# A spatial bias added by TensorE instead of VectorE, with the gate product moved from GpSimd to VectorE

## The chip, the cores and the metric

The kernel runs on one core of one Trainium2 chip. The metric is the device time of one execution in microseconds (us). Of the kernel before, three runs are shown: 330.44, 331.29 and 336.69 us, median 331.29. One further execution was profiled; it took 327.45 us, of which 325.7 us lie between its first and its last instruction (the span).

The engines that matter are TensorE (PE: matmuls; PEld: its weight loads), VectorE (DVE), ScalarE (ACT), GpSimd (POOL), and SyncE's queue (SP), which issues nearly all DMAs. Each engine carries out its instructions in order.

## The reference

Three blocks follow each other, each in float32, for a batch of 2 with 768 positions and a model width of 320:

1. an mLSTM attention (8 heads of 40) with exponential gates, computed in the kernel in 6 chunks of 128 positions for each batch;
2. a gated MLP with a spatial product, the block that is changed:

```
h = relu(x @ w_in);  u, v = h[..., :512], h[..., 512:]
v_n = (v - mean(v)) / sqrt(var(v) + 1e-6)
v_s = einsum('ts,bsd->btd', w_spatial, v_n) + b_spatial[None, :, None]
out = (u * v_s) @ w_out
```

3. a channel mix: two blends of x with its predecessor in time, `k = relu(xk @ w_k)**2`, `sigmoid(xr @ w_r) * (k @ w_v)`.

The bias `b_spatial` belongs to an output position t and is the same for every batch and channel.

## The kernel before, in words

**High and low parts.** Matmuls take operands of a type (float32r) that holds less than a float32. Every operand is therefore kept as a high part (a rounding copy, made on ScalarE) and a low part (the value minus the high part, made by the helper `sub` in line 232 on VectorE or GpSimd). A product is then three matmuls: high by high, high by low, low by high. Weights that arrive as raw bits go through `widen` (lines 248 to 286): a step on ScalarE (L269), three on VectorE (L270, L274, L278), the high part on ScalarE (L285), the low part on GpSimd (L232).

**Stages.** The attention runs chunk by chunk; in its gaps the v and u halves of the first product of block 2 are computed, as "fillers". `vpart` leaves the normalised v as `vn` (high and low), `upart` leaves u transposed as `ut`. When the last chunk is through, the pool `at` of the attention is released (line 964), and two pools take its memory over: `rk`, with 3 buffers "sq" and 11 buffers "gk" (`gated`), and `r1`, with `b_sb` (the bias, broadcast to 128 partitions) and the second half of w_spatial.

**The spatial stage** is written out in line 1084: `'h s0 K1 s1 r o0 K0 s2 v x o1 s3 o2'`. `s0` to `s3` are the groups g (batch g // 2, half g % 2 of the output positions, 384 of them). A group has four chunks d of 128 channels, and `spatial(g, d)` gives each one PSUM bank of 128 channels by 384 positions: 6 blocks of input positions, three products each, 18 matmuls. `after` queues the chain of the gate: add the bias (VectorE, L999), multiply by u (GpSimd, L1000), high part (ScalarE, L1001), low part (VectorE, L232). `o0` to `o3` are `wout(g)`, the output projection of a group into a page `x2`; `K0`, `K1`, `r` and `v` queue the widening of w_k, w_r and w_v; `x` makes the blend xk of group 0. After that come, for each group, `kpart` (tiles kp, k), rp and vv; `wout(3)` stands after the fourth `kpart` of group 0.

**What sets the order.** A planner runs in Python while the kernel is built. It keeps a clock for TensorE and a time at which each other engine comes free (`free`), gives every step of a chain a cost in us, and issues the step that can start first; `use` books time on an engine for an instruction issued outside of a chain. The result is a fixed order on TensorE, ScalarE, VectorE and GpSimd. SP's DMAs are ordered by the framework. The planner's costs are estimates: a real wait on one engine does not move the order on another. Work of `widen` counts as late and steps back behind chains that are ready.

**Memory.** There are 8 PSUM banks; a matmul into a bank waits until the bank's last reader is through. Pages ("pg", 12 of them) are handed round: a page for `x2` may be one from which `vn` is still read.

Of the kernel before, what the change touches and what calls it, by code (L numbers as in the profile page):

```python
# [7 lines left out]
F32 = mybir.dt.float32  # L8
F32R = mybir.dt.float32r
# [4 lines left out]
ALU = mybir.AluOpType  # L14
# [3 lines left out]
def tile_mlstm_gmlp_channelmix(  # L18
# [26 lines left out]
    P = 128  # L45
    H, D = 8, 40
    DA = D + 1
    B, S = 2, 768
# [4 lines left out]
    HF = 384  # L53
# [4 lines left out]
    vec, act, pool, pe = nc.vector, nc.scalar, nc.gpsimd, nc.tensor  # L58
# [64 lines left out]
    def use(e, cost, t=None):  # L123
        free[e] = max(free[e], clock[0] if t is None else t) + cost
        return free[e]
# [44 lines left out]
    def chain(key, *steps, ready=None):  # L170
        running.append(Chain(key, steps, clock[0] + 0.2 if ready is None else ready, 0.0))

    def finish(*keys, stall=True):
        for k in keys:
            while any(b[0] == k or b[0][0] == k for b in back):
                if not force_feed():
                    break
            for c in [c for c in running if c.has(k)]:
                while c in running and c.has(k):
                    advance(c.start(), skip=c)  # L180
                    if not c.open():
                        finish(split[0], stall=False)
                    if c in running and c.has(k):
                        issue(c)
        if stall:
            at_least(max([done.get(k, 0.0) for k in keys], default=0.0))
# [18 lines left out]
    def own(tag, bufs, *keys):  # L205

        h = owners.setdefault(tag, [])
        if len(h) >= bufs:
            finish(*h[-bufs], stall=tag in ("at", "mm"))
        h.append(list(keys))  # L210
# [20 lines left out]
    def sub(eng, out, a, b):  # L231
        eng.tensor_tensor(out=out, in0=a, in1=b.bitcast(F32), op=ALU.subtract)  # L232
# [82 lines left out]
    def load_qk(i):  # L315
        b, c = divmod(i, NCH)
        t = at.tile([P, 2, 4, P], F32, tag="qk", name=f"qk{i}", bufs=2)
        for hh in range(2):
            e = load(t[64 * hh:64 * hh + D], qk[b, c, hh], 164)
        st["q", i], st["k", i] = t[:, 0], t[:, 1]  # L320
        st["at", i] = e
# [11 lines left out]
    def load_o(u):  # L333
        b, j = divmod(u, 2)
        o = at.tile([P, 3, DM], F32, tag="og", name=f"og{u}", bufs=3)
        load(o, o_tok[b, j], 480)
        st["o", u] = o
# [13 lines left out]
    for a in 'i f d o2 o0 q'.split():  # L351
        dict(f=lambda: sync.dma_start(out=fg, in_=f_gate), i=lambda: sync.dma_start(out=ig, in_=i_gate),
             d=lambda: sync.dma_start(out=id_sb, in_=ident), o=lambda: load_o(int(a[1])), q=lambda: load_qk(SEQ[0]))[a[0]]()
# [290 lines left out]
    def mm_bank(name, *keys):  # L644
        if closing:
            closing.append(0)
            if len(closing) % 4:
                return bank(psa, "at", name, *keys)
        return bank(psm, "mm", name, *keys)
# [3 lines left out]
    ut = {}  # L653
# [268 lines left out]
    while todo:  # L922
        p = todo[0]["p"]
# [46 lines left out]
    def gated(name):  # L970
        return rk.tile([P, 2, HF], F32R, tag="gk", name=name, bufs=11)

    r1 = tc.alloc_tile_pool(name="r1", bufs=1, side="right", reuse_waits="tile")
    b_sb = r1.tile([P, S], F32, name="b_sb")
    sync.dma_start(out=b_sb, in_=b_sp)
    x2 = {}
    gts = {}

    def run(prs, out, after, first=(), cost=0.16):
        for t in mm3([out], prs, after, first, cost):  # L980
            t[0]()

    def spatial(g, d):
        b, hf = divmod(g, 2)
        prs = []
        for s in range(NCH):
            v0, v1 = (t[:, s % 3, d * P:(d + 1) * P] for t in vn[2 * b + s // 3])
            w = W["sp", hf][s // 3]
            w0, w1 = w[:, 0, s % 3, :], w[:, 1, s % 3, :]
            prs += [(v0, w0), (v0, w1), (v1, w0)]  # L990

        def after(ps):
            own("sq", 3, ("gt", g, d))
            vs = rk.tile([P, HF], F32, tag="sq", name=f"vs{g}_{d}", bufs=3)
            gt = gated(f"gt{g}_{d}")
            sl = slice(hf * HF, (hf + 1) * HF)
            finish(*[("ut", b, 3 * b + j, d) for j in range(3)], stall=False)
            chain(("gt", g, d),
                  ("V", 0.47, lambda: vec.tensor_tensor(out=vs, in0=ps, in1=b_sb[:, sl], op=ALU.add), ("sp", g, d)),  # L999
                  ("P", 0.96, lambda: pool.tensor_tensor(out=vs, in0=vs, in1=ut[b][:, d, sl], op=ALU.mult)),  # L1000
                  ("A", 0.41, lambda: act.copy(gt[:, 0], vs)), ("V", 0.47, lambda: sub(vec, gt[:, 1], vs, gt[:, 0])))  # L1001
            gts[g, d] = gt

        run(prs, mm_bank(f"spp{g}_{d}", ("sp", g, d))[:, :HF], after, [f"w_sp{hf}"] + [("vn", NCH * b + s) for s in range(NCH)])
# [62 lines left out]
    def sp_run(g):  # L1067
        for d in range(4):
            spatial(g, d)
# [39 lines left out]
    for g in range(2 * B):  # L1109
# [8 lines left out]
        for j in range(3):  # L1118
            sl = slice(j * P, (j + 1) * P)
# [6 lines left out]
        for j in range(3):  # L1126
            sl = slice(j * P, (j + 1) * P)
            prs = []
# [119 lines left out]
```

## Time and profile before

| | us |
|---|---|
| runs shown (3) | 330.44, 331.29, 336.69 |
| median | 331.29 |
| the profiled execution | 327.45 |
| its span | 325.7 |
| TensorE busy | 302.4 (93%) |
| VectorE busy | 224.3 (69%) |
| ScalarE busy | 163.2 (50%) |
| GpSimd busy | 145.6 (45%) |

Times in the rows below are us from the start of the span. A timeline row gives start, duration, engine, line and operation, the tiles (written <- read), shape and count; in square brackets stands how long the engine had been idle just before and what released it. Matmuls are pipelined, and the durations of several overlap: the pitch of a row of matmuls is its duration divided by its count. The granted clock of TensorE has two levels, 1.2 and 2.4 GHz, shown as 0.50 and 1.00.

### The profile page before, as it was taken

The numbers are of one execution on the slowest core, as the hardware profiler recorded it, in microseconds if no ns is written. First come the engines' busy times: TensorE is split into PE (matmuls) and PEld (weight loads), VectorE is DVE, ScalarE is ACT, GpSimd is POOL, SyncE is SP. The second block draws the span as 40 slices with busy tenths as digits, with TensorE's granted clock in tenths as the row PEclk, the third lists the DMA queues.
The fourth block names the chain that finished last, engine by engine and source line by source line (L and its number), as shares of the span: only waits on it lengthen the run. The fifth ranks groups of instructions, "written<-read, shape, count | busy, mean of one in ns | idle before, by whom it ended". The sixth has DMA issues, their size and how long they took to land.

```text
span 325.7 us, 5486 instructions
## 1 busy us (share of the span) xinstructions
PE 302.4 (93%) x1982; PEld 281.5 (86%) x1982; DVE 224.3 (69%) x430; ACT 163.2 (50%) x336; POOL 145.6 (45%) x185
## 2 busy tenths in 40 slices
PE   5979988999999999899999999449999999999995
PEld 3676866989989989799999999339999999999995
DVE  6679698958689656654997929996565745645611
ACT  4542644685466342742455316458874844753620
POOL 4133457935758644853464631655502502501500
PEclk9969997999999999999999999987999999999999
DMA  5763942353443213244115211410001001001001
GB/s 181 248 174 124 344 135 85 109 169 105 163 132 112 84 49 104 89 155 139 42 40 193 83 40 40 122 42 2 0 22 41 2 20 40 2 20 42 0 20 42
DMA packets 12854, 28.97 MB, mean 89 GB/s; under 512 B 2099, under 2 KB 6187, under 8 KB 12827
## 3 DMA queue, kind: packets, MB, share of 16 engines
q1 hardware_dynamic: 12795, 28.56, 27.5%
q8 instruction: 16, 0.26, 0.3%
q14 instruction: 11, 0.09, 0.1%
q0 software_dynamic: 32, 0.07, 0.1%
HBM read 26.35 MB, written 1.97 MB: 87 GB/s over the span
## 4 chain that ended last, share of the span: by engine, by line
PE 74%; DVE 10%; ACT 5%; POOL 4%; DMA 3%; issue 2%; SPq 1%; DVEq 0%; ACTq 0%; POOLq 0%
PE spp L612 14%; PE vv L612 13%; PE kp L612 12%; PE vp L612 6%; PE wop L612 5%; PE up L612 5%; PE av L541 5%; PE rp L612 4%; PE sc L444 3%; DMA w_inv<-in_w_in_dram 2%; PE ld L453 2%; DVE wbits L274 2%; PE wp L348 2%; PE ip L525 2%; PE sp L491 1%
## 5 line engine op out<-in xcount | busy, mean ns | idle before, releaser
L1101 POOL TENSOR_TENSOR sq<-sq 128x384 f32<-128x384 f32 x32 | 27.2, 852 | 60.3 <-ACT sq L1100 60.3
L612 PE MATMUL spp<-wsp,vn 128*128 128x384 f32 x288 | 51.0, 335 | 1.5 <-POOL vn L232 0.9
L612 PEld LDWEIGHTS spp<-wsp,vn 128*128 128x128 f32 x288 | 49.8, 188 | 2.2 <-POOL vn L232 1.2
L612 PE MATMUL kp<-xk,wk 128*128 128x384 f32 x256 | 45.9, 336 | 4.6 <-DVE vs L999 4.6
L612 PEld LDWEIGHTS kp<-xk,wk 128*128 128x128 f32 x256 | 44.4, 188 | 5.2 <-DVE vs L999 5.2
L612 PE MATMUL vv<-wv,k 128*128 128x320 f32 x288 | 43.4, 310 | 0.1
L612 PEld LDWEIGHTS vv<-wv,k 128*128 128x128 f32 x288 | 42.4, 188 | 0.6 <-DVE k L232 0.3
L232 DVE TENSOR_TENSOR k<-sq,k 128x384 fp32r<-128x384 f32 x32 | 25.7, 802 | 21.7 <-ACT k L1102 21.7
L612 PE MATMUL vp<-w_v,xg 128*128 128x512 f32 x96 | 29.3, 422 | 2.3 <-ACT xg L603 1.4
L612 PE MATMUL up<-xg,w_u 128*128 128x256 f32 x192 | 31.2, 293 | 0.0
L612 PE MATMUL wop<-gt,wo 128*128 128x384 f32 x128 | 25.7, 358 | 4.5 <-DVE vs L999 2.9
L612 PEld LDWEIGHTS wop<-gt,wo 128*128 128x128 f32 x128 | 24.1, 203 | 5.7 <-ACT wv L285 3.2
L1000 POOL TENSOR_TENSOR vs<-vs,u 128x384 f32<-128x384 f32 x16 | 20.5, 1281 | 14.2 <-DVE vs L999 14.2
L612 PEld LDWEIGHTS up<-xg,w_u 128*128 128x128 f32 x192 | 26.2, 190 | 0.5
L541 PEld LDWEIGHTS av<-kvq,dt 128*128 128x128 f32 x192 | 25.7, 203 | 0.7
L541 PE MATMUL av<-kvq,dt 128*128 128x41 f32 x192 | 25.3, 284 | 0.0
L1100 ACT ACTIVATE sq<-kp 128x384 f32<-128x384 f32 x32 | 15.4, 491 | 15.4 <-PE kp L612 15.4
L274 DVE SCALAR_TENSOR_TENSOR wbits<-wsq,wbits 128x320 int32<-128x320 int32 (+1 forms) x27 | 21.3, 793 | 2.5 <-ACT wsq L269 2.1
L612 PEld LDWEIGHTS vp<-w_v,xg 128*128 128x128 f32 x96 | 17.5, 194 | 5.8 <-DVE xg L232 1.5
L466 DVE TENSOR_TENSOR dt<-dt,sc 128x512 f32<-128x512 f32 x24 | 16.2, 682 | 7.7 <-ACT dt L463 4.5
L1140 DVE TENSOR_TENSOR ob<-rs,vv 128x320 f32<-128x320 f32 x12 | 5.8, 487 | 20.7 <-PE vv L612 20.7
L463 ACT ACTIVATE dt<-ld 128x512 f32<-128x512 f32 x24 | 14.1, 597 | 9.2 <-PE ld L455 6.1
(160 smaller groups left out, 560.3 us busy)
## 6 DMA issues: line engine op xcount, KB each, us to landing
kvq<-in_kvq_dram SPq DMA_DIRECT2D x10, 516.0 KB
qk<-in_qk_dram SPq DMA_DIRECT2D x24, 160.0 KB
wraw<-in_w_k_dram SPq DMA_DIRECT2D x6, 512.0 KB
wraw<-in_w_v_dram SPq DMA_DIRECT2D x8, 320.0 KB
wraw<-in_w_sp_dram SPq DMA_DIRECT2D x12, 192.0 KB
og<-in_o_tok_dram SPq DMA_DIRECT2D x4, 480.0 KB
out_dram<-ob SPq DMA_DIRECT2D x12, 160.0 KB
w_inv<-in_w_in_dram SPq DMA_DIRECT2D x3, 512.0 KB
```

The source lines that it names most:

```text
L232: eng.tensor_tensor(out=out, in0=a, in1=b.bitcast(F32), op=ALU.subtract)
L274: vec.scalar_tensor_tensor(out=t["bits"], in0=t["sq"].bitcast(I32), scalar=3, in1=t["bits"], op0=ALU.logical_shift_left, op1=ALU.bitwise_or)
L348: pe.matmul(wp[:, :256], junk[:, :P], junk, start=True, stop=True)
L444: pe.matmul(st["sc", i, x][:, h * P:(h + 1) * P], k_[64 * x:64 * x + D, h, :], q_[64 * x:64 * x + D, h, :], start=True, stop=True)
L453: pe.matmul(ld, lts[c % 2][:, b], rl[:, hh * 512:(hh + 1) * 512], start=True, stop=not early)
L463: ("A", 0.48, lambda: act.activation(out=d2, in_=ld, func=AF.Exp), ("e", i, hh)),
L466: ("V", 0.6, lambda: vec.tensor_tensor(out=d2, in0=d2, in1=sc, op=ALU.mult)))
L541: pe.matmul(av[:, 4 * hh + h, :], A[:, h, :], vt[:, 4 * hh + h, :], start=True, stop=True)
L612: pe.matmul(out[0], l, x, start=j == 0, stop=j == len(prs) - 1)
L1000: ("P", 0.96, lambda: pool.tensor_tensor(out=vs, in0=vs, in1=ut[b][:, d, sl], op=ALU.mult)),
L1100: chain(("k2", g, f), ("A", 0.37, lambda: act.activation(out=sq, in_=ps, func=AF.Relu), ("kp", g, f)), ("P", 0.96, lambda: pool.tensor_ten ...
L1101: ("P", 0.96, lambda: pool.tensor_tensor(out=sq, in0=sq, in1=sq, op=ALU.mult)),
```

## The change

The bias becomes a 19th matmul of every chunk. Its moving operand is `bm`, 128 rows of 768 positions: the first 64 rows hold the high part of the bias, the last 64 rows the low part. Its stationary operand `sel` is 1/64 everywhere, so that the sum over the 128 rows is high part plus low part, for each of the 128 channels. `b_sb` is loaded into the first "gk" buffer; ScalarE makes the high part for all rows, VectorE subtracts it in the lower 64 rows. VectorE multiplies the PSUM bank by u directly; GpSimd has no step in the chain any more. The two calls of `use` book 0.85 and 0.9 us in the planner.

```diff
     r1 = tc.alloc_tile_pool(name="r1", bufs=1, side="right", reuse_waits="tile")
-    b_sb = r1.tile([P, S], F32, name="b_sb")
+
+
+    b_sb = gated("b_sb").rearrange("p w t -> p (w t)").bitcast(F32)
+    bm = r1.tile([P, S], F32R, name="bm")
+    sel = r1.tile([P, P], F32R, name="sel")
     sync.dma_start(out=b_sb, in_=b_sp)
+    pool.memset(sel.bitcast(F32), 1.0 / 64)
+    act.copy(bm, b_sb)
+    sub(vec, bm[64:], b_sb[64:], bm[64:])
+    use("A", 0.85)
+    use("V", 0.9)
     x2 = {}
     gts = {}
...
             prs += [(v0, w0), (v0, w1), (v1, w0)]
+        prs.append((sel, bm[:, hf * HF:(hf + 1) * HF]))
...
             chain(("gt", g, d),
-                  ("V", 0.47, lambda: vec.tensor_tensor(out=vs, in0=ps, in1=b_sb[:, sl], op=ALU.add), ("sp", g, d)),
-                  ("P", 0.96, lambda: pool.tensor_tensor(out=vs, in0=vs, in1=ut[b][:, d, sl], op=ALU.mult)),
+                  ("V", 0.55, lambda: vec.tensor_tensor(out=vs, in0=ps, in1=ut[b][:, d, sl], op=ALU.mult), ("sp", g, d)),
                   ("A", 0.41, lambda: act.copy(gt[:, 0], vs)), ("V", 0.47, lambda: sub(vec, gt[:, 1], vs, gt[:, 0])))
```

## Rows read from the trace of the kernel before

**Rows 1.** Page, part 1: busy us, share of the span, instructions of TensorE

```profile
PE 302.4 (93%) x1982; PEld 281.5 (86%) x1982; DVE 224.3 (69%) x430; ACT 163.2 (50%) x336; POOL 145.6 (45%) x185
```

**Rows 2.** Page, part 4: the chain of waits, by engine

```profile
PE 74%; DVE 10%; ACT 5%; POOL 4%; DMA 3%; issue 2%; SPq 1%; DVEq 0%; ACTq 0%; POOLq 0%
```

**Rows 3.** Timeline, TensorE, start of the spatial stage

```profile
133.85 2.77 PE L612 MATMUL spp<-wsp,vn 128*128 128x384 f32 x15
...
137.27 0.62 PE L612 MATMUL spp<-wsp,vn 128*128 128x384 f32 x2 [0.65 <-ACT vn L681]
...
138.75 21.43 PE L612 MATMUL spp<-wsp,vn 128*128 128x384 f32 x122 [0.87 <-POOL vn L232]
```

**Rows 4.** Timeline, TensorE alone, group 2 and the output projection of group 3

```profile
166.44 12.64 PE L612 MATMUL spp<-wsp,vn 128*128 128x384 f32 x72
...
216.29 1.72 PE L612 MATMUL wop<-gt,wo 128*128 128x384 f32 x6 [2.94 <-DVE vs L999]
...
220.27 6.19 PE L612 MATMUL wop<-gt,wo 128*128 128x384 f32 x25 [0.93 <-DVE gt L232]
```

**Rows 5.** Timeline, ScalarE and VectorE at the release of x2

```profile
195.41 0.48 ACT L1018 COPY x<-wop 64x384 f32<-64x384 f32 x1 [6.69 <-PE spp L612]
...
195.92 0.55 DVE L1019 TENSOR_TENSOR x<-x,wop 64x384 f32<-64x384 f32 x1 [6.77 <-ACT x L1018]
...
197.03 0.55 DVE L232 TENSOR_TENSOR gt<-vs,gt 128x384 fp32r<-128x384 f32 x1
```

**Rows 6.** Timeline, SP: issue of b_sb's transfer

```profile
138.00 0.43 SPq L975 DMA_DIRECT2D b_sb<-in_b_sp_dram  x1
```

**Rows 7.** Stretches: us; busy PE, PEld, DVE, ACT, POOL; PEclk, DMA share, GB/s

```profile
138.00:140.50 2.50, 1.75 (x10) 1.75 (x11) 0.95 (x1) 0.62 (x4) 2.42 (x5) 1.00 0.74 243
140.50:142.50 2.00, 2.00 (x13) 2.00 (x12) 0.94 (x1) 1.86 (x4) 1.45 (x2) 1.00 0.00 0
```

**Rows 8.** Timeline, ScalarE and GpSimd, last steps of the attention's vn

```profile
140.49 0.62 ACT L681 CAST vn<-vr 128x512 fp32r<-128x512 f32 x1 [1.88 <-DVE vr L679]
...
141.19 1.31 POOL L232 TENSOR_TENSOR vn<-vr,vn 128x512 fp32r<-128x512 f32 x1 [0.55 <-ACT vn L681]
```

**Rows 9.** Tile vs: count, duration ns min/median/max, first and last start

```profile
L999 DVE TENSOR_TENSOR vs<-spp,b_sb x16: 543/546/558, 143.4 to 215.6; 128x384 f32<-128x384 f32 x16
L1000 POOL TENSOR_TENSOR vs<-vs,u x16: 1007/1293/1462, 144.1 to 216.8; 128x384 f32<-128x384 f32 x16
L1001 ACT CAST gt<-vs x16: 495/512/520, 146.3 to 218.1; 128x384 fp32r<-128x384 f32 x16
```

**Rows 10.** Timeline, a wider cast on ScalarE and a subtraction of 768 columns

```profile
198.91 1.16 ACT L1044 CAST xk<-tm 128x1152 fp32r<-128x1152 f32 x1 [0.57 <-DVE tm L1040]
...
226.01 0.96 DVE L232 TENSOR_TENSOR xr<-tm,xr 128x768 fp32r<-128x768 f32 x1 [0.44 <-ACT xr L1044]
```

**Rows 11.** Timeline of 211 to 222, VectorE and GpSimd, w_v split and gate

```profile
211.76 1.20 POOL L1000 TENSOR_TENSOR vs<-vs,u 128x384 f32<-128x384 f32 x1 [1.20 <-DVE vs L999]
212.01 1.30 DVE L278 SCALAR_TENSOR_TENSOR wsq<-wraw,wbits 128x320 int32<-128x320 int32 x1
...
213.82 0.49 DVE L278 SCALAR_TENSOR_TENSOR wsq<-wraw,wbits 128x320 int32<-128x320 int32 x1
...
214.23 0.98 DVE L270 TENSOR_SCALAR wbits<-wraw 128x320 int32<-128x320 int32 x1
...
215.60 0.55 DVE L999 TENSOR_TENSOR vs<-spp,b_sb 128x384 f32<-128x384 f32 x1
...
219.66 0.55 DVE L232 TENSOR_TENSOR gt<-vs,gt 128x384 fp32r<-128x384 f32 x1
```

**Rows 12.** Stretches, columns as in rows 7

```profile
53.10:56.40 3.30, 3.30 (x20) 2.69 (x17) 3.13 (x7) 1.12 (x2) 2.25 (x4) 0.50 0.01 3
213.50:216.80 3.30, 0.51 (x3) 0.54 (x4) 3.20 (x6) 2.04 (x5) 1.97 (x2) 1.00 0.33 99
217.00:223.60 6.60, 5.03 (x15) 4.12 (x14) 5.51 (x11) 5.20 (x12) 3.00 (x4) 0.50 0.01 4
```

## The prediction

> **What bounds the kernel now.** I read the busy shares first: TensorE is busy for 302.4 us of the span of 325.7 [rows 1]. The chain of waits agrees, with TensorE at 74% and VectorE at 10% [rows 2]. So an added matmul costs its whole pitch nearly everywhere, and the question is where the VectorE tenth lies. The timelines show two regimes around the change.
>
> Up to 203 us the spatial stage is TensorE's. After its last wait at 138.75 it runs without a gap, 72 spatial matmuls in 12.64 us [rows 3, 4], a pitch of 0.176 us.
>
> Then the bound changes hands. ScalarE's copy into x2 of group 1 waits 6.69 us and is let go at 195.41 by a spatial matmul of group 3, nine before that group's end: x2's page is one that the spatial products still read. VectorE stands behind it, idle for 6.77 us [rows 5]. When both are let go, VectorE has 24 us of queued work, does it almost without a pause, and TensorE waits for its PSUM banks (2.94 us at 216.29) and for the last split of the gate, running freely again from 220.27 [rows 4]. I call 195.4 to 220.3 the VectorE stretch. The change touches both sides.
>
> **The change, part by part**
>
> *Sixteen more matmuls*, one per group and half-chunk, each 128x384 like the others: 16 x 0.176 = **+2.8 us**. TensorE is the bound there, so nothing covers them; their weight load is one more in a stream whose loads already overlap.
>
> *The preparation of the bias, and its new wait.* Before, b_sb was needed only by VectorE's first addition. Now the 19th matmul of the first group needs bm, made by a DMA, a ScalarE cast and a VectorE subtraction. TensorE's order is fixed, so all products queue behind that one. When does it ask? The first 15 matmuls start at 133.85, two at 137.27, the 18th at 138.75 [rows 3], so the 19th is up at 138.93. When is bm there? The b_sb transfer is issued at 138.00, behind a w_sp transfer in SP's queue [rows 6]; the DMA engines are 0.74 busy to 140.50 and at 0.00 afterwards [rows 7], so it has landed by 140.50. I keep that time: the new buffer is again one of a pool that opens after the attention's last instructions. ScalarE then casts the last vn from 140.49 to 141.11 [rows 8]. The copy of 128x768 follows: 0.51 us for 384 columns [rows 9], 1.16 for 1152 [rows 10], so 0.84, done at 141.9. The subtraction of 768 columns takes 0.96 [rows 10], done at 142.9 if nothing holds it. But GpSimd's vn subtraction runs from 141.19 to 142.50 [rows 8], and a VectorE operation that meets GpSimd here takes until GpSimd's end and most of its own time: 1.30 us against 0.49 for the same form [rows 11]. That puts bm at 143.4. TensorE waits from 138.93 to 143.4: **+4.5 us** (between 4.0, without the collision, and 5.5, with 1 us more for the transfer). No later slack takes it up, since TensorE has no gap until 203.
>
> The Trainium skill ("SBUF — State Buffer", Who interferes with whom) states the same as an exclusive lock: a VectorE instruction with two SBUF inputs blocks against a GpSimd instruction that reads SBUF. By it the later of the two times holds; without it the sum would be 0.5 us less.
>
> The sel memset on GpSimd comes behind that vn subtraction, at 142.5, and has 0.9 us before bm is ready. If it were slower it would be the late one. The w_sp casts and splits of the second half queue behind copy and subtraction, about 2 us later; their products begin 72 matmuls after the first half's, and these are themselves 4.5 us later: nothing.
>
> *What the pause does to TensorE's clock.* In 53.1 to 56.4 the granted clock was 0.50 for 3.3 us; after a stretch with TensorE idle in 2.8 of 3.3 us it was 0.50 for 6.6 us [rows 12]. A 4.5 us pause is nearest to the second, which followed the longer idleness; part of the slow time falls into the pause itself, so I take 5 us of matmuls at half speed, which loses **+2.5 us** (0.9 to 3.3).
>
> The Trainium skill ("TensorE: Matmul & The Clock Gate", HAM oscillation) speaks against this change: it charges a gap in the matmul stream a slow restart on top. Without that the sum would be 2.5 us lower; rows 12 side with the rule.
>
> *The addition becomes a multiplication on VectorE*, again one PSUM and one SBUF input of 128x384. The addition took 543 to 558 ns in all 16 cases [rows 9], also where GpSimd was busy: **0** (within 0.02 each).
>
> *GpSimd loses 16 products* of 1.0 to 1.46 us [rows 9]. In the spatial stage this shortens only a chain that nobody waits for. In the VectorE stretch four remain, and each collides with a step of the w_v split, as in the product at 211.76 with the step at 212.01 [rows 11]; the four excesses are 0.64 to 0.83 us, the one shown 0.81. Three lie ahead of what TensorE waits for: **-2.3 us** (0 if the w_v subtractions of GpSimd move into the freed place and collide there; -3.1 for all four).
>
> *Order on VectorE.* The planner writes each engine's order. Without the GpSimd step the cast and the split of a gate follow their multiplication about 1.1 us sooner in its plan. The split of group 2's last chunk, at 197.03 [rows 5], then comes ahead of the wait for x2, where VectorE is idle: **-0.5 us**. At the end, the last addition starts at 215.60 and the last gate's split at 219.66, with four operations and a GpSimd product between [rows 11]; TensorE starts 0.6 us after the split starts. Directly behind one operation and ScalarE's 0.51 us cast the split would end about 2.2 us after the multiplication starts; now it ends 4.6 us after. **-2.5 us** (0 to -3.5). What is late next is TensorE's own queue: 25 products of the output projection and 32 of kp, about 10 us, then rp, whose input VectorE makes after the same stretch.
>
> *Sum against the profiled execution* (327.45 us; span 325.7 and 1.75 around it): 2.8 + 4.5 + 2.5 - 2.3 - 0.5 - 2.5 = +4.5, so 331.9. The runs shown have a median of 331.29 us, 3.8 above the profiled execution; on that median I forecast **335.7 us**. TensorE is the bound from 220.3 to the end, so the difference passes through.
>
> **The rivals**
>
> *R1, no pause.* If SP issues the b_sb transfer some 5 us earlier, bm is ready at 138.9 and pause and slow clock vanish: 2.8 - 5.3 = -2.5, **328.8 us**. For it: the transfer waits in SP's queue, not for its source. Against: it now stands directly behind a w_sp transfer, and nothing in the edit takes it out of there.
>
> *R2, the stretch does not shrink (slower).* VectorE is full in 195.4 to 220.3 with or without the products, and only what stands between the last multiplication and the last split counts. If the planner fills the freed GpSimd time with w_v splits, these keep colliding and keep their places, and only the 0.5 is won: 2.8 + 4.5 + 2.5 - 0.5 = +9.3, **340.6 us**. It decides once less than 3.1 of the 5.3 us come back, for then the sum passes the 2% limit of +6.6. For it: eight w_v subtractions on GpSimd stay, and one costs VectorE the same as a product, as at 214.23 with 0.98 us [rows 11]. Against: the four shown collisions are with the products.
>
> *R3, a later transfer (slower).* The new buffer may lie over memory that the attention's last chain still reads until 142.50 [rows 8]. Then the transfer of 2.5 us starts there, the cast is done at 145.9 and bm, without collision, at 146.8: a pause of 7.9 us, and 2.8 + 7.9 + 3.3 - 5.3 = +8.7, **340 us**. Against: the buffer is the first one of its pool, and most of what lay there has been read long before.
>
> *R4, more comes back.* In the stretch TensorE also loses to the half clock of 217 to 223.6 [rows 12], with 5.0 us busy, so 2.5 us. If shorter waits keep the clock up, the forecast becomes +2.0, **333.3 us**.
>
> **How the numbers follow.** The forecast gets 0.50, R1 0.15, R2 0.16, R3 0.10, R4 0.09. A measurement of this kernel can tell about 2%, here 6.6 us: under 324.7 is faster, over 337.9 slower. R2, R3 and the upper end of the forecast (longer pause, full slow time) give slower 0.28. Faster needs R1 and R4 together with a little more: 0.06. Within 2%: 0.66. The range reaches from R1 to R2, 328.8 to 340.6; the forecast's own, with its bounds, is 332 to 339.
>
> **What would show it.** Right: TensorE waits at the first bias product for VectorE's split of bm, 4 to 5 us, and a clock of 0.5 follows; the steps of the w_v split in the last stretch stay under 0.6 us unless a w_v subtraction overlaps; the last gate split starts within 2.5 us of the last multiplication. Wrong: no wait in front of the first bias product (R1), one of 7 us or more behind the DMA (R3), or a distance from the release of x2 to the last wait of the output projection that is still near 24.9 us (R2).

## The result, and the profile after

The changed kernel takes 334.18 us, the kernel before 331.17 (medians of 20 runs each). Some executions of each kernel are longer at a lower granted clock; ratios, here and below, leave these out, so they are not the quotients of the medians. The ratio is 1.0117, with a 95% interval of 1.0079 to 1.0156: 3.9 us slower (2.6 to 5.2), where +4.5 was forecast. It is within 2%.

The profiled execution of the changed kernel took 339.42 us with a span of 337.7. In the attention, which the change does not touch, TensorE ran at half clock for 17 us in one piece (53.0 to 70.1), where the kernel before had 3.3 us [rows 12]. Such pieces differ between executions of one kernel: the repeat of the changed kernel has 6.8 us there (50.7 to 57.5). So spans are not compared below: I count from the 18th spatial matmul of group 0, the last one ahead of the place where the change begins.

The page's busy times and the chain of waits of the changed kernel:

```profile
PE 313.2 (93%) x1998; PEld 292.2 (87%) x1998; DVE 215.4 (64%) x431; ACT 163.9 (49%) x337; POOL 126.6 (37%) x170
...
PE 70%; DVE 11%; ACT 7%; issue 4%; DMA 3%; POOL 3%; SPq 1%; DVEq 0%; ACTq 0%; POOLq 0%
```

Against [rows 1] TensorE has 16 matmuls more and GpSimd 19 us less. VectorE did not gain on the chain [rows 2]: 11% instead of 10%.

**The first bias product.** The timeline of the changed kernel, all engines:

```profile
144.30 0.43 SPq L979 DMA_DIRECT2D b_sb<-in_b_sp_dram  x1
...
145.06 0.44 PE L612 MATMUL spp<-wsp,vn 128*128 128x384 f32 x1 [0.86 <-POOL vn L232]
...
147.48 1.30 POOL L232 TENSOR_TENSOR vn<-vr,vn 128x512 fp32r<-128x512 f32 x1 [0.55 <-ACT vn L681]
147.58 0.83 ACT L981 CAST bm<-b_sb 128x768 fp32r<-128x768 f32 x1 [0.18 <-DMA b_sb<-in_b_sp_dram]
...
148.44 1.15 DVE L232 TENSOR_TENSOR bm<-b_sb,bm 64x768 fp32r<-64x768 f32 x1 [1.69 <-ACT bm L981]
148.70 0.22 POOL L980 MEMSET sel<- 128x128 f32 x1
149.74 0.66 PE L612 MATMUL spp<-bm,sel 128*128 128x384 f32 x1 [4.24 <-DVE bm L232]
150.19 5.67 PE L612 MATMUL spp<-wsp,vn 128*128 128x384 f32 x18
...
155.87 3.28 PE L612 MATMUL spp<-wsp,vn 128*128 128x384 f32 x18
```

The row of 149.74 shows it: the bias product waits, and what lets it go is VectorE's split of bm, behind the transfer, ScalarE's cast of 0.83 us and the end of GpSimd's vn subtraction. By the pitch the next product was up at about 145.25, so the pause is 149.74 - 145.25 = 4.49 us. Behind it 19 matmuls take 155.70 - 149.74 = 5.96 us, where 18 later ones take 3.28 instead of 5.67. Later rows of 18 with their bias product start 3.29 to 3.30 us apart, a pitch of 0.174; at it 19 take 3.30, so 2.66 us are lost. The stretches show why (columns as in rows 7):

```profile
145.25:149.74 4.49, 0.25 (x2) 0.03 (x1) 2.08 (x2) 2.69 (x5) 3.12 (x5) 0.87 0.33 121
150.20:153.50 3.30, 3.30 (x12) 3.30 (x12) 2.43 (x5) 0.52 (x1) 0.00 (x0) 0.50 0.29 80
...
230.00:234.00 4.00, 4.00 (x13) 3.44 (x14) 2.33 (x6) 2.89 (x7) 1.75 (x2) 0.57 0.01 2
```

The granted clock falls late in the pause (at 148.6; its mean there is 0.87) and stays at 0.50, the lower level, until 155.4, while TensorE is busy without a gap. The third stretch belongs to the next part.

**The VectorE stretch.** ScalarE, VectorE and GpSimd of the changed kernel, from the last split of group 2 to the last split of group 3 (the rows of 216.44 to 223.25 and of 227.94 are read further down):

```profile
195.69 0.56 DVE L232 TENSOR_TENSOR gt<-vs,gt 128x384 fp32r<-128x384 f32 x1
...
211.37 0.48 ACT L1027 COPY x<-wop 64x384 f32<-64x384 f32 x1 [15.71 <-PE spp L612]
211.87 0.55 DVE L1028 TENSOR_TENSOR x<-x,wop 64x384 f32<-64x384 f32 x1 [15.10 <-ACT x L1027]
...
216.44 1.00 DVE L270 TENSOR_SCALAR wbits<-wraw 128x320 int32<-128x320 int32 x1
...
221.05 1.00 DVE L270 TENSOR_SCALAR wbits<-wraw 128x320 int32<-128x320 int32 x1
...
223.25 0.98 DVE L270 TENSOR_SCALAR wbits<-wraw 128x320 int32<-128x320 int32 x1
...
225.67 0.87 POOL L232 TENSOR_TENSOR wv<-wsq,wv 128x320 fp32r<-128x320 f32 x1 [1.62 <-ACT wv L285]
225.90 0.99 DVE L278 SCALAR_TENSOR_TENSOR wsq<-wraw,wbits 128x320 int32<-128x320 int32 x1
...
227.94 0.95 DVE L270 TENSOR_SCALAR wbits<-wraw 128x320 int32<-128x320 int32 x1
...
229.22 0.54 DVE L1009 TENSOR_TENSOR vs<-spp,u 128x384 f32<-128x384 f32 x1
...
231.16 0.55 DVE L232 TENSOR_TENSOR gt<-vs,gt 128x384 fp32r<-128x384 f32 x1
```

And TensorE alone:

```profile
222.97 1.67 PE L612 MATMUL kp<-xk,wk 128*128 128x384 f32 x8 [1.41 <-DVE vs L1009]
226.03 1.69 PE L612 MATMUL kp<-xk,wk 128*128 128x384 f32 x8 [1.39 <-DVE vs L1009]
...
229.91 7.57 PE L612 MATMUL wop<-gt,wo 128*128 128x384 f32 x32 [2.19 <-ACT wv L285]
237.31 5.71 PE L612 MATMUL kp<-xk,wk 128*128 128x384 f32 x32
...
250.62 1.59 PE L612 MATMUL vv<-wv,k 128*128 128x320 f32 x7 [1.01 <-ACT k L1111]
```

The split of group 2 stands ahead of the wait for x2, VectorE's multiplication of a PSUM bank takes 0.54 us, and the last split starts 231.16 - 229.22 = 1.94 us after the last multiplication, where 219.66 - 215.60 = 4.06 lay between before [rows 11]. The step at 225.90 still lasts 0.99 us: now it meets GpSimd's subtraction of w_v. TensorE's wait that ends at 229.91 is again one for a PSUM bank: VectorE's last multiplication ends at 229.76, and ScalarE's cast, which the row names, at 229.79, but this product does not read it. The 32 products then run in one row, so TensorE no longer waits for the last split; the granted clock is 0.50 from 230.5 to 233.9.

All kernels of this study, counted in this way. "18th" is the start of the 18th spatial matmul, "release" ScalarE's copy into x2, "kp5" the run of 32 kp matmuls that follows the stretch, and the end is the span's:

| kernel | 18th to release | release to kp5 | kp5 to end | sum |
|---|---|---|---|---|
| before | 56.66 | 30.89 | 99.40 | 186.95 |
| after | 66.31 | 25.94 | 100.39 | 192.64 |
| changed again | 66.10 | 25.82 | 100.55 | 192.47 |
| bias last in group 0 | 60.82 | 25.72 | 100.61 | 187.15 |
| the same again | 60.84 | 25.71 | 100.65 | 187.20 |
| product on GpSimd | 66.16 | 31.10 | 98.86 | 196.12 |
| no bias | 58.22 | 24.80 | 101.92 | 184.94 |
| fillers in the pause | 65.52 | 27.96 | 98.89 | 192.37 |
| group 3 in two passes | 55.66 | 26.24 | 99.66 | 181.56 |
| useless GpSimd product | 65.65 | 29.51 | 99.18 | 194.34 |

The change loses 9.65 us ahead of the release, takes 4.95 back in the stretch and gives 0.99 up again behind it.

### The profile page after: what moved, and what is told of

Same layout as the page of the kernel before. It is cut to its first block, busy times and chain, and to the rows that moved or that the text cites. A ratio compares the mean times of both kernels' runs of the same rounds, so it can differ in the third digit from the quotient of the medians.

```text
span 337.7 us, 5498 instructions
## 1 busy us (share of the span) xinstructions
PE 313.2 (93%) x1998; PEld 292.2 (87%) x1998; DVE 215.4 (64%) x431; ACT 163.9 (49%) x337; POOL 126.6 (37%) x170
## 4 chain that ended last, share of the span: by engine, by line
PE 70%; DVE 11%; ACT 7%; issue 4%; DMA 3%; POOL 3%; SPq 1%; DVEq 0%; ACTq 0%; POOLq 0%
PE spp L612 15%; PE vv L612 12%; PE kp L612 10%; PE vp L612 6%; PE av L541 5%; PE up L612 5%; PE wop L612 3%; PE rp L612 3%; PE sc L444 3%; DMA w_inv<-in_w_in_dram 2%; PE ld L453 2%; PE ip L525 2%; DVE wsq L278 2%; PE sp L491 2%; PE wp L348 2%
## 5 line engine op out<-in xcount | busy, mean ns | idle before, releaser
L612 PE MATMUL spp<-wsp,vn 128*128 128x384 f32 x288 | 55.4, 346 | 1.5 <-POOL vn L232 0.9
L612 PEld LDWEIGHTS spp<-wsp,vn 128*128 128x128 f32 x288 | 52.6, 197 | 2.2 <-POOL vn L232 1.2
L612 PE MATMUL up<-xg,w_u 128*128 128x256 f32 x192 | 32.8, 303 | 0.0
L612 PEld LDWEIGHTS up<-xg,w_u 128*128 128x128 f32 x192 | 27.8, 200 | 0.6
L541 PEld LDWEIGHTS av<-kvq,dt 128*128 128x128 f32 x192 | 27.4, 215 | 0.8
L541 PE MATMUL av<-kvq,dt 128*128 128x41 f32 x192 | 26.9, 295 | 0.0
L612 PE MATMUL wop<-gt,wo 128*128 128x384 f32 x128 | 24.7, 351 | 2.2 <-ACT wv L285 2.2
L274 DVE SCALAR_TENSOR_TENSOR wbits<-wsq,wbits 128x320 int32<-128x320 int32 (+1 forms) x27 | 18.0, 670 | 2.7 <-ACT wsq L269 2.4
L232 POOL TENSOR_TENSOR wk<-wsq,wk 128x512 fp32r<-128x512 f32 x6 | 8.8, 1467 | 28.5 <-ACT wk L285 28.5
L232 POOL TENSOR_TENSOR wv<-wsq,wv 128x320 fp32r<-128x320 f32 x8 | 8.0, 1004 | 29.7 <-ACT wv L285 29.7
```

Source lines behind the costliest of these rows:

```text
L274: vec.scalar_tensor_tensor(out=t["bits"], in0=t["sq"].bitcast(I32), scalar=3, in1=t["bits"], op0=ALU.logical_shift_left, op1=ALU.bitwise_or)
L541: pe.matmul(av[:, 4 * hh + h, :], A[:, h, :], vt[:, 4 * hh + h, :], start=True, stop=True)
L612: pe.matmul(out[0], l, x, start=j == 0, stop=j == len(prs) - 1)
```

## The experiments

Each kernel is the changed one with the edit shown, against the kernel before on the same chip. Medians: of the kernel before 332.55 us beside the first four and 333.04 beside the others.

**Bias last in group 0.** The four bias products of group 0 follow its 72 other products, so bm is ready long before.

```diff
-        run(prs, mm_bank(...)[:, :HF], after, ...)
+        r = mm3([mm_bank(...)[:, :HF]], prs, after, ...)
+        for t in r if g else r[:-1]:
+            t[0]()
+        return r[-1][0]
...
-        for d in range(4):
-            spatial(g, d)
+        tails = [spatial(g, d) for d in range(4)]
+        for t in tails if g == 0 else ():
+            t()
```

> Only the place of four matmuls moves: in group 0 the four bias products come after the 72 spatial products instead of one behind each chunk. Theory (the changed kernel loses some 7 us because its first bias product waits 4.5 us for bm and TensorE then runs at half clock): the wait is gone, no half clock follows it, ratio to the kernel before 0.99 (0.985 to 0.997), that is 7 us under the changed kernel. Rival (the time goes into the sixteen products and the new order, the wait would be covered by slack further on): about 1.01 as for the changed kernel. A further rival, for the move itself: four gate chains start together at the end of group 0 and hold up group 1, then TensorE waits for banks in group 1.

Measured: 329.58 us, ratio 0.9994 (0.9917 to 1.007). TensorE of this kernel, and the stretch behind its last short wait:

```profile
136.25 11.39 PE L612 MATMUL spp<-wsp,vn 128*128 128x384 f32 x55 [0.86 <-POOL vn L232]
147.48 0.85 PE L612 MATMUL spp<-bm,sel 128*128 128x384 f32 x4
...
215.61 7.34 PE L612 MATMUL wop<-gt,wo 128*128 128x384 f32 x32 [2.22 <-ACT wv L285]
...
236.32 8.04 PE L612 MATMUL vv<-wv,k 128*128 128x320 f32 x51 [1.23 <-ACT k L1115]
...
138.00:140.00 2.00, 2.00 (x8) 2.00 (x8) 0.51 (x1) 1.98 (x4) 1.45 (x3) 0.50 0.03 7
```

The wait for bm is gone and 66.31 - 60.82 = 5.49 us come back ahead of the release. That is the pause of 4.49 and 1.0 us of slow clock, not 2.7: without the pause TensorE still runs at half clock, for 3.4 us from 137.1 on, behind nothing longer than the short waits that close the attention (0.86 us in the first row). Behind the stretch another 1.2 us are lost against the kernel before (100.61 and 99.40). So the kernel is level with the one before and not 1% under it, and my expectation failed there.

**Product on GpSimd.** The bias stays on TensorE; VectorE only copies the bank and GpSimd multiplies, as before.

```diff
-                  ("V", 0.55, lambda: vec.tensor_tensor(out=vs, in0=ps, in1=ut[b][:, d, sl], op=ALU.mult), ("sp", g, d)),
+                  ("V", 0.47, lambda: vec.tensor_copy(vs, ps), ("sp", g, d)),
+                  ("P", 0.96, lambda: pool.tensor_tensor(out=vs, in0=vs, in1=ut[b][:, d, sl], op=ALU.mult)),
```

> Bias on TensorE as in the change, but the product with u goes back to GpSimd: VectorE copies the bank out, GpSimd multiplies. Theory (5 us come back in the stretch after the release of x2 because GpSimd's four products no longer stand against VectorE and in front of the last split): they are lost again, from the release of x2 to TensorE's last wait 24 to 25 us instead of 18.5, ratio 1.03 (1.024 to 1.034). Rival R2 (the w_v subtractions collide as much, the stretch does not depend on the products): ratio 1.01 as for the changed kernel.

Measured: 339.16 us, ratio 1.026 (1.0203 to 1.0317). ScalarE's copy and TensorE:

```profile
210.34 0.48 ACT L1028 COPY x<-wop 64x384 f32<-64x384 f32 x1 [9.92 <-PE spp L612]
...
226.68 1.68 PE L612 MATMUL kp<-xk,wk 128*128 128x384 f32 x8 [2.68 <-DVE vs L1009]
...
231.08 1.28 PE L612 MATMUL wop<-gt,wo 128*128 128x384 f32 x6 [2.71 <-DVE vs L1009]
...
241.44 5.71 PE L612 MATMUL kp<-xk,wk 128*128 128x384 f32 x32
```

With the product back on GpSimd the stretch is 31.10 us, that of before (30.89), and the waits for the banks are back. All that the stretch gave came from moving the product. R2, that it would not shrink, falls.

**No bias.** The bias is left out altogether (b_sb, bm, sel and the 16 products); the product stays on VectorE.

```diff
-    sync.dma_start(out=b_sb, in_=b_sp)
-    pool.memset(sel.bitcast(F32), 1.0 / 64)
-    act.copy(bm, b_sb)
-    sub(vec, bm[64:], b_sb[64:], bm[64:])
...
-        prs.append((sel, bm[:, hf * HF:(hf + 1) * HF]))
```

> The bias is left out altogether (no load, no bm, no bias products); the gate product stays on VectorE straight from PSUM. So this is the second half of the change alone. Theory: no pause, no sixteen products, and the stretch shrinks by 5 us: ratio 0.985 (0.980 to 0.990). Rival R2: 0.995 to 1.0.

Measured: 325.33 us, ratio 0.986 (0.9815 to 0.9905). TensorE and ScalarE's copy:

```profile
137.46 23.87 PE L612 MATMUL spp<-wsp,vn 128*128 128x384 f32 x127 [0.86 <-POOL vn L232]
...
195.68 0.48 ACT L1017 COPY x<-wop 64x384 f32<-64x384 f32 x1 [13.19 <-PE spp L612]
...
235.18 8.04 PE L612 MATMUL vv<-wv,k 128*128 128x320 f32 x51 [1.82 <-ACT k L1101]
```

Against "bias last" 60.82 - 58.22 = 2.60 us are gone ahead of the release. Fifteen of the 16 products lie there (four in each of groups 0 to 2, three in group 3): 15 x 0.174 = 2.6. Each costs its pitch.

**Fillers in the pause.** TensorE gets 42 matmuls that nobody uses, ahead of the first bias product.

```diff
...
+        if g == d == 0:
+            junk, wp = id_sb.bitcast(BF16), psm.tile([P, 512], F32, tag="mm", name="wp")
+            for _ in range(42):
+                pe.matmul(wp[:, :256], junk[:, :P], junk, start=True, stop=True)
+        r[-1][0]()
```

> The changed kernel, with 42 unused matmuls of 128x256 bf16 (about 4.5 us) in front of the first bias product, so that TensorE works while it would wait. Theory: the wait itself stays (its 4.5 us are filled), the half clock behind it does not come: 2.5 us under the changed kernel, ratio 1.004 (1.000 to 1.008). Rival (the half clock has another cause, such as the many weight loads): ratio unchanged at 1.01 and a granted clock of 0.5 behind the first bias product.

Measured: 332.61 us, ratio 1.0103 (0.9984 to 1.0222), inconclusive. TensorE, and two stretches:

```profile
138.82 6.41 PE L1019 MATMUL wp<-id_sb 128*128 128x256 bf16 x42
...
144.98 0.42 PE L612 MATMUL spp<-bm,sel 128*128 128x384 f32 x1
145.24 3.31 PE L612 MATMUL spp<-wsp,vn 128*128 128x384 f32 x18
...
140.00:141.00 1.00, 1.00 (x7) 0.69 (x6) 0.22 (x1) 0.62 (x1) 0.45 (x2) 0.50 0.35 133
145.00:146.00 1.00, 1.00 (x9) 1.00 (x7) 0.56 (x2) 0.00 (x0) 0.00 (x0) 1.00 0.00 0
```

Behind the fed pause the clock is 1.00 and 18 matmuls take 3.31 us instead of 5.67. But the granted clock was at its lower level from 138.8 to 142.2, as in the kernels without the pause, and this fell on the fillers: they took 6.41 us, and the bias product started at 144.98 although bm was ready at 143.05. So only 0.8 us are won up to the release. The stretch is 2.0 us longer than the changed kernel's, with 6.8 us at half clock in it instead of 3.4, and 1.5 us come back behind it. The ratio misses the expected 1.004, with an interval too wide to tell the two apart.

**Group 3 in two passes.** Built on "bias last": in group 3 the first 9 products of each chunk run ahead of the other 10 of every chunk. The blocks that keep x2's page are then read earlier, and the same matmuls run in another order.

```diff
...
     def sp_run(g):
+        cut = {0: 18, 3: 9}.get(g, 19)
+        rest = []
         for d in range(4):
-            spatial(g, d)
+            r = spatial(g, d)
+            for t in r[:cut]:
+                t[0]()
+            rest += r[cut:]
+        for t in rest:
+            t[0]()
```

> Group 0 as in e1 (its four bias products last), and group 3 in two passes: the nine products of the first three input blocks for all four chunks first, then the rest. x2's page is read by the first pass only, so it is released some 6 us earlier while TensorE still has 40 matmuls. Theory (TensorE's waits in the stretch hang on the moment of that release): from group 3's end to the next free run TensorE waits 3 us or less instead of 5, and what is won there is given back in part at vv, which waits for k; ratio to the kernel before 0.985 (0.975 to 0.993), under e1. Rival (the stretch is bound by VectorE's amount of work after the banks fill, not by the release): as e1, 0.99, with the waits moved but not shorter.

Measured: 325.70 us, ratio 0.9913 (0.9855 to 0.997), faster than the kernel before, and than the changed kernel beside it (1.0192). ScalarE's copy, and TensorE:

```profile
195.50 0.48 ACT L1027 COPY x<-wop 64x384 f32<-64x384 f32 x1 [9.02 <-PE spp L612]
...
213.09 1.66 PE L612 MATMUL kp<-xk,wk 128*128 128x384 f32 x8 [0.35 <-DVE vs L1009]
214.92 1.46 PE L612 MATMUL wop<-gt,wo 128*128 128x384 f32 x7 [0.17 <-DVE vs L1009]
217.29 4.61 PE L612 MATMUL wop<-gt,wo 128*128 128x384 f32 x25 [0.92 <-DVE x L1033]
```

The release comes 60.82 - 55.66 = 5.2 us sooner, VectorE begins its queue sooner, and TensorE's waits in the stretch shrink from 5.0 to 1.6 us (the three shown and one of 0.15). So the release of x2 starts the stretch, as [rows 5] were read. Two more things come back: the granted clock stays at 1.00 from 195 to 222, so the 1.7 us that the half clock cost "bias last" there are saved, and the wait at vv, which I had expected to grow, is 0.25 us instead of 1.23.

**A useless GpSimd product.** The changed kernel, with a product of 128x300 on GpSimd beside each gate that nobody waits for. It brings back the collisions and leaves the chain of the gate as short as the change made it.

```diff
...
+            def gate():
+                vec.tensor_tensor(out=vs, in0=ps, in1=ut[b][:, d, sl], op=ALU.mult)
+                chain(("by", g, d), ("P", 0.96, lambda: pool.tensor_tensor(
+                    out=spare, in0=vs[:, :300], in1=ut[b][:, d, sl][:, :300], op=ALU.mult)),
+                    ready=max(clock[0], free["V"]) + 0.7)
...
-                  ("V", 0.55, lambda: vec.tensor_tensor(out=vs, in0=ps, in1=ut[b][:, d, sl], op=ALU.mult), ("sp", g, d)),
+                  ("V", 0.55, gate, ("sp", g, d)),
```

> The changed kernel with a useless product on GpSimd beside each gate (128x300 of the same operands into a spare tile), on which no step waits. So the collisions with VectorE come back and the chain stays short. Theory: the two parts of the 5 us are separate, the collisions are worth 2 to 3 us: from the release of x2 to the start of the fifth kp 28 us (26 without, 31 with the products in the chain), ratio 1.02 (1.014 to 1.026). Rival (only the shorter chain and the new order count): 26 us and the ratio of the changed kernel. Other rival (only the collisions count): 31 us and 1.027.

Measured: 339.2 us, ratio 1.0302 (1.0197 to 1.0406); the changed kernel beside it has 1.0192. ScalarE's copy, VectorE's last multiplication, and one stretch:

```profile
206.71 0.48 ACT L1035 COPY x<-wop 64x384 f32<-64x384 f32 x1 [12.90 <-PE spp L612]
...
225.69 0.55 DVE L1011 TENSOR_TENSOR vs<-spp,u 128x384 f32<-128x384 f32 x1
...
224.30:234.40 10.10, 8.54 (x25) 7.26 (x24) 7.26 (x14) 6.81 (x15) 4.46 (x5) 0.50 0.01 2
```

From the release to the last multiplication it needs 225.69 - 206.71 = 18.98 us, the changed kernel 229.22 - 211.37 = 17.85. The lengthened steps of VectorE there have an excess of 4.4 us (three beside the useless products, four beside w_v subtractions), as in the kernel before and 1.3 more than in the changed one. So the collisions cost 1.1 us there. The rest of the 3.6 us by which this stretch is longer comes with a half clock that lasts 10.2 us instead of 3.4; whether the collisions brought that about is open. With it the stretch (29.5 us, 28 expected) and the ratio (1.026 at most expected) came out longer than I had said.

**Two repeats.** "Bias last" and the changed kernel ran again beside these two.

> e1 once more beside the changed kernel on one chip. Theory: 0.99 to the kernel before and 5 to 7 us under e8. Rival: the same as e8.

> The changed kernel itself, as the reference for e5 to e7 on one chip: ratio 1.012 (1.005 to 1.018), a wait of 4 to 5 us for bm and a half clock behind it that lasts as long as before or longer than 3 us.

Measured: 330.04 us, 1.0038 (0.997 to 1.0105), and 333.85 us, 1.0192 (1.0143 to 1.0241). By the two ratios the pause and what follows it cost 1.5%, 5 us, and the trace says the same with 192.47 - 187.20 = 5.3. Their intervals against the kernel before overlap with those of the first runs. Two expectations were missed by the ratios: 1.0038 for 0.99, as in the first run, and 1.0192 for at most 1.018.

## Why the forecast held, step by step

| term | forecast | measured |
|---|---|---|
| 16 products | +2.8 | +2.8 (15 of them 2.60) |
| pause for bm | +4.5 | +4.49 |
| half clock behind the pause | +2.5 | +2.66, of it about 1.0 from the pause alone (see below) |
| multiplication on VectorE | 0 | 0 (0.54 to 0.56 us, as the addition) |
| release to last gate step | -2.8 (-2.3 and -0.5) | -2.34 |
| last gate step to its split | -2.5 | -2.12 |
| half clock in the stretch | 0 (R4: -2.5) | about -0.8 |
| behind the stretch | 0 | +1.0 |
| sum | +4.5 | +5.7 in the trace; +3.9 timed |

The mechanism held, and that the sum came so near is in part luck. The collisions gave back 1.0 us less than forecast and the wait behind the stretch cost 1.0 more; a shorter half clock in the stretch (0.8) and the new order on VectorE (1.0, of which 0.5 was forecast) made up for most of it.

**The pause** came as worked out, with one link read differently: ScalarE's cast was let go by the transfer, 2.52 us after the 18th matmul started, and not by the vn cast in front of it. I had put it at 141.11 - 138.75 = 2.36. The split met GpSimd's subtraction and took 1.15 us where I had 1.5 with the collision and 0.96 without. GpSimd ended at 148.78, 0.34 us into the split, which became 0.19 us longer than the 0.96 of [rows 10]. The eight kernels with a bias, the repeats among them, show what that means: the overlap was 0.15 to 0.54 us, the split 0.01 to 0.40 us longer, always 0.14 to 0.15 less than the overlap. The Trainium skill ("SBUF — State Buffer", Who interferes with whom) calls the port pair that the two engines share an exclusive lock. The traces agree but for that constant: the split loses one for one what it overlaps.

**The half clock** has the size of the forecast, but it is not all the pause's. The four kernels without the pause ("bias last" twice, "no bias", "two passes") each show 3.4 us at half clock in the same place, behind waits that the kernel before has too [rows 3], while its profile shows 1.00 from 138 to 142.5 [rows 7]. The four with an unfilled pause show 6.8 us each, but more or less of it falls into the pause: the 19 matmuls behind it lost 2.66 us in the changed kernel, 2.47 in its repeat, 2.51 in "product on GpSimd" and 1.66 beside the useless product, where the kernels without the pause lost 1.7. So the pause alone adds 0 to 1.0 us. One execution cannot tell whether the kernel before is usually spared. If it is not, the change costs about 1.5 us less than the trace makes it, and the difference between 5.7 in the trace and 3.9 timed would be of that size. This was not shown, and the timed repeat, with 1.0192 or about 6.3 us, speaks against it.

**The collisions** are the term that was mis-sized: the step "three lie ahead of what TensorE waits for: -2.3" took the four products away and left GpSimd's other work as harmless as it had been. Between release and last gate step the kernel before has seven lengthened steps of the w_v split, the changed one five (216.44 to 227.94 above). Those of the kernel before, with 212.01 and 214.23 of [rows 11]:

```profile
203.52 1.14 DVE L270 TENSOR_SCALAR wbits<-wraw 128x320 int32<-128x320 int32 x1
204.76 0.98 DVE L274 SCALAR_TENSOR_TENSOR wbits<-wsq,wbits 128x320 int32<-128x320 int32 x1
...
207.82 1.12 DVE L278 SCALAR_TENSOR_TENSOR wsq<-wraw,wbits 128x320 int32<-128x320 int32 x1
208.87 0.98 DVE L270 TENSOR_SCALAR wbits<-wraw 128x320 int32<-128x320 int32 x1
210.08 0.67 DVE L270 TENSOR_SCALAR wbits<-wraw 128x320 int32<-128x320 int32 x1 [0.23 <-DMA wraw<-in_w_v_dram]
```

Against their unhindered length (0.32 and 0.48 us) that is an excess of 4.45 us before (0.82, 0.50, 0.64, 0.66, 0.35, 0.82, 0.66) and of 3.16 after (0.68, 0.68, 0.66, 0.51, 0.63): 1.3 us, and 1.1 by the useless product. What was left out is the lower bound's own reason, that w_v subtractions move and collide anew, as at 225.90: steps beside them alone had an excess of 2.2 us before and have 3.2 now. The remaining 1.0 us of the 2.34 comes with the new order, and not from fewer steps. Group 2's split went ahead of the wait, as forecast, and with it two steps of the blend; three steps of the w_v split moved in behind the release, so that VectorE carries out 33 steps there before and after. About 0.3 us of it is idle time of VectorE (1.27 us before, 0.95 after).

**The last split** ends 231.16 + 0.55 - 229.22 = 2.49 us after the last multiplication starts; 2.2 was forecast, and 4.6 was read before. Two w_v steps still stand between, one of them, again beside GpSimd, of 0.98 us.

**Rivals.** R1, no pause, and R3, one of 7.9 us, fall on the row of 149.74. R2 falls on its own sign, the distance from the release to the last wait of the output projection (229.91 - 211.37 = 18.5 us, 24.9 before), and on "product on GpSimd"; the amount at which it was to decide is 9.8 - 6.6 = 3.2 us and not 3.1, and nothing hangs on that. R4 came in part: in the stretch TensorE was busy for 5.0 us at half clock before [rows 12] and for 3.4 after (from 230.5), which lose 2.5 and 1.7. In "no bias" and "two passes" the stretch has no half clock at all.

**Not foreseen: the wait behind the stretch.** I let the difference pass from kp5 to the end. But ScalarE's cast of the last k starts 250.07 - 211.37 = 38.70 us after the release, where it started 42.66 after it before (238.07 - 195.41):

```profile
238.07 0.50 ACT L1102 CAST k<-sq 128x384 fp32r<-128x384 f32 x1
```

It came forward by 3.96 us and TensorE's queue by 4.95. The difference of 0.99 is spent at vv: the 22nd matmul of that row starts 1.31 us behind the 21st, in the kernel before 0.33 (0.15 is its pitch). Of the others, "bias last" has this wait with 1.23, "no bias", with the shortest stretch, with 1.82, "product on GpSimd", with the long one, not at all.

## What to carry to other kernels

An operand that a stage only needs at its end, such as a bias that is accumulated, belongs at the end of the accumulation: as the 19th product of the first bank it stopped an engine that works in order for the whole latency of transfer, cast and split (4.5 us, and 5 to 5.5 with the clock), as the last product of the group it cost its pitch alone. Taking work from an engine beside which another's steps become longer can give back less than the collisions that it was seen in, since the rest of its work moves and collides instead: 1.3 of 2.3 us here. And look for what starts a crowded stretch before shortening its steps: another order of the same matmuls, which let a page go 5.2 us sooner, took "bias last" from +0.4% to -0.9% on the same chip.

## What the runs showed of the hardware beside that

- The granted clock fell to its lower level (1.2 GHz) also behind short waits: in "bias last", 3.4 us at 0.50 followed a wait of 0.86 us, with TensorE busy from then on, while the one profile of the kernel before shows 1.00 behind the same waits. With the pause of 4.49 us it was 6.8 us, from 148.6, within the pause, on.
- A matmul of this form costs 0.174 us at full clock whether it belongs to a group of 18 or is the one added behind it: 15 more took 2.60 us.
